# One broadcast per quad, another prologue order, early scaling of wo and wider FFN chunks in a transformer block on one core

## The chip, the cores and the metric

The kernel runs on one core of a Trainium2 chip. The core has a matrix engine (TensorE, PE in the profile), three engines for elementwise work (VectorE or DVE, ScalarE or ACT, GpSimd or POOL) and a queue engine (SyncE or SP) that issues transfers. TensorE writes its results into eight accumulator banks of 128 x 512 32-bit numbers (PSUM); everything else lives in the on-chip memory. The metric is the device time of one execution in microseconds (us); lower is better.

## The reference

One adaLN-conditioned transformer block over 2048 tokens of width 512, with 32 heads of 16 columns, and a gated FFN of width 1792:

```python
mod = (silu(c) @ w_mod).reshape(1, 6, 1, 512)        # sa, ca, ga, sb, cb, gb
h = layernorm(x) * (1 + ca) + sa
q, k, v = split_heads(h @ wqkv)                      # 32 heads, 16 columns each
p = softmax(q @ k.T * 16 ** -0.5)                    # 2048 x 2048 for each head
x = x + ga * (merge_heads(p @ v) @ wo)
h = layernorm(x) * (1 + cb) + sb
x = x + gb * ((gelu(h @ w_gate) * (h @ w_up)) @ w_down)
```

The 32 x 2048 x 2048 exponentials of the softmax are the bulk of the elementwise work.

## The kernel before

**Units and rounds.** Queries are cut into seven sets of 512, 512, 256, 256, 256, 128 and 128 tokens (`SETS`, L33). Heads are taken four at a time: a quad is the four heads that stand in the four 32-row groups of one 128-row slice, the even or the odd ones (`kme` and `kmo` hold the keys with the other heads' rows set to zero). A unit is a set and a quad; the last two sets share their first five quads. A unit is computed as the transposed scores of 128 keys by W queries; a block is 128 x 512 scores of one head. There are 2048 blocks.

**The stream** (`stream`, L1052). Six accumulator banks form two halves of three. TensorE fills one half with score blocks (`qk`), while ACT turns the other half into bf16 exponentials in one instruction of up to 1536 columns (L1167). In some rounds one of the three blocks is given to DVE instead, which computes 2 to a power by integer and polynomial steps in seven instructions (`exp_vec`, L1235): a load `dt` out of the accumulator bank, `dx`, two scalings, two products and a last combining step. ACT's instruction is then 1024 columns wide. The test that gives a block to DVE is at L1147: fewer than three such blocks under way, fewer than ten ready DVE steps in the backlog, and a side credit below 2600 (1600 near the end).

Sixteen rows of values and a column of ones (`vaug`) follow as the other product (`pv_mms`), so that each head's sum of exponentials comes out beside its output. At the end of a unit (`pv_done`, L1295), DVE copies the result to `osb`; the sums of the quad go to a scratch tensor in device memory and come back spread over all partitions (`den`); DVE takes reciprocals (`rden`); they go out to scratch again and come back as a broadcast over 32 partitions per head, in `rb`: four transfers issued by SP, each with a semaphore of its own. Then DVE multiplies `osb` by `rb` into `onorm`.

**Side work.** Projections of later slices, the output projection (`side_wo`), and the FFN of finished sets (`side_ffn`) are cut into small pieces and put between the score products. `plan` (L978) lists them with a start and a due position, and a credit lets them in. A piece of side work that waits for a DVE step holds the rest of the list. `side_ffn` computes the gate, x + 0.044715 x cubed on DVE, a tanh on ACT, the up projection, and the product, in chunks of two or more slices of 128 hidden columns (`width`, L870).

**The planner.** The program is written out ahead of time for every engine. `model` (L245) keeps a clock for each engine, with costs from `cost` (L284); each next instruction is chosen by what could run at that time. A step of DVE is put into DVE's order when its inputs are ready in this clock (`step`, L945). What the clock has wrong, the engines find out as waits, because each engine runs its instructions in the written order.

**The prologue** (`prologue`, L488) is written out by hand: loads, a warm-up of TensorE, statistics of the first tiles, `ln_rstd` on POOL (an addition and a power), normalisation on DVE, modulation columns, transposes, modulation by DVE and ACT, and K and Q of the first 512 tokens. **The tail** (`tail`, L1339) handles the last sets: `tail_den`, `tail_end` and `tail_ffn`.

**wo.** `scale_wo` (L791) multiplies the output weights by `ga` late, after the last but one set's second normalisation; earlier sets apply `ga` in `wo_fin` (L806), in a product and an addition.

Of the kernel before, what the change touches and what calls it, by code (L numbers as in the profile page):

```python
# [6 lines left out]
ALU = mybir.AluOpType  # L7
# [7 lines left out]
P = 128  # L15
# [63 lines left out]
class _Recorder:  # L79
# [165 lines left out]
    def model(self, op, t, cost):  # L245
        eng = op.eng
        if op.stream not in COMPUTE:
            self.free[eng] = t + (430 if eng == "sp" else 50)
            self.dma_free = max(t + 800, self.dma_free) + cost / 350
            op.t1 = self.dma_free + 1000  # L250
        elif eng == "pe":
            cols, rows, tp = cost
            mode = 0 if tp is None else (1 if rows == 32 else 2)
            t = max(t, self.pe_issue)
            if mode != self.pe_mode:
                t = max(t, self.pe_end + 105)
# [27 lines left out]
    def cost(self, eng, out, ins, kind):  # L284
# [6 lines left out]
        if eng == "act":  # L291
            return n * 0.833 + (51 if ps else 93)
        if eng == "pool":
            return n * (30.0 if n <= 4 else 3.0) + 200
        f = 1
# [17 lines left out]
    def act(self, out, in_, func, bias=None, scale=1.0, accum=None):  # L313
        kw = {} if bias is None else {"bias": bias}
        wr = [out]
        if accum is not None:
# [3 lines left out]
        return self.rec("act", lambda e: e.activation(out, in_, func, scale=scale, **kw), rd, wr,  # L320
                        cost=self.cost("act", out, [in_], "act"))

# [89 lines left out]
class _Kernel(_Recorder):  # L412
# [75 lines left out]
    def prologue(self):  # L488
# [30 lines left out]
        self.ts(dve, self.rm[:, 0:1], self.rm[:, 1:2], -1.0, 1.0, ALU.mult, ALU.add)  # L519

        for dc in range(NDC):
            self.mm(self.scp[:, 0, dc:dc + 1], self.crow[0:1, P * dc:P * dc + P], self.ones[0:1, 0:1])
# [10 lines left out]
        self.ln_rstd(0, 4)  # L533
        self.memset(pool, self.vaug[:, :, :].rearrange("p t (h c) -> p t h c", c=VW)[:, :, :, DH:VW], 1.0)
        self.mod_cols(self.scp[:, 1, 0:8], 0)
# [5 lines left out]
        for dc in range(NDC):  # L541
            pt = self.scp[:, 2 + dc, :].bitcast(BF16)[:, 0:512]
            for t in range(4):
                self.transpose(pt[:, P * t:P * t + P], self.tb1[:, 0, t, P * dc:P * dc + P], self.ident[:, :])
            self.modulate(dve if dc % 2 == 0 else act, self.hT[:, dc, 0:512], pt, self.modA, dc)
        for t in range(6, 8):
            self.ln_stat(t)
        self.proj_k(0, 0, self.scp[:, 2, :], "both")
        self.proj_q(0, 0, self.scp[:, 3, :], act)
        self.act_stat_fin(4, 6)  # L550
# [20 lines left out]
    def ln_rstd(self, a, b):  # L571
        r = self.rstd[:, a:b]
        self.ts("pool", r, self.mv[:, a:b, 1], EPS, None, ALU.add)
        self.tt("pool", r, r, self.half[:, 0:b - a], ALU.pow)

# [27 lines left out]

    def proj_k(self, g, dc, bank, how):
        self.proj(bank, 512 + P * dc, g)
        sl = slice(512 * g, 512 * g + 512)
        if how == "both":
            self.act(self.km[1][:, dc, sl], bank, ACT.Copy, scale=self.rm[:, 1:2])
        else:
            self.ts("dve", self.km[1][:, dc, sl], bank, self.rm[:, 1:2], None, ALU.mult)  # L610
        self.ts("dve", self.km[0][:, dc, sl], bank, self.rm[:, 0:1], None, ALU.mult)

    def proj_q(self, g, dc, bank, eng):
# [4 lines left out]
        else:  # L618
            self.ts(eng, out, bank, Q_SCALE, None, ALU.mult)

    def proj_v(self, g, dc, bank):
        for t in range(4):
            for dci in range(NDC):
                self.mm(bank[:, P * t:P * t + P], self.hT[:, dci, 512 * g + P * t:512 * g + P * t + P],
                        self.wqkv[:, dci, 1024 + P * dc:1024 + P * dc + P],
                        start=(dci == 0), stop=(dci == NDC - 1))
        dst = self.vaug[:, 4 * g:4 * g + 4, VW * 8 * dc:VW * 8 * dc + VW * 8]
        self.copy("dve", dst.rearrange("p t (h c) -> p t h c", c=VW)[:, :, :, 0:DH],
                  bank.rearrange("p (t h c) -> p t h c", t=4, c=DH))

# [160 lines left out]
    def scale_wo(self):  # L791

        if not self.dry:
            self.task([lambda qd=qd: self.tt("dve", self.wo[:, qd, :], self.wo[:, qd, :], self.ga[:, :], ALU.mult)
                       for qd in range(8)], "wo", self.after([("ln2", len(SETS) - 2)]))
        return
        yield

# [7 lines left out]
    def wo_fin(self, bank, t):  # L806
        return [lambda: self.tt("dve", self.xw[:, :], bank, self.ga[:, :], ALU.mult),
                lambda: self.tt("dve", self.xs[:, t, :], self.xs[:, t, :], self.xw[:, :], ALU.add)]

# [47 lines left out]
    def side_ffn(self, gi, part=None):  # L857
# [11 lines left out]
        chunks = []  # L869
        width = max(2, kpb)  # L870
        for a in range(0, NFC, width):
# [106 lines left out]
    def plan(self, ends, nsplit):  # L978
# [6 lines left out]
        w.append((lambda: self.side_dc(1), at(30), at(51)))  # L985
        w.append((self.side_mod, at(50), at(59)))
        w.append((lambda: self.side_dc(2), at(59), at(90)))
        w.append((lambda: self.side_q_all(1), at(90), at(105)))
# [12 lines left out]
        w.append((lambda: self.side_wo(k), s0, s0))  # L1001
        w.append((self.scale_wo, s0, s0))
        w.append((lambda: self.side_ffn(k, EARLY), s0, n - 20))
# [291 lines left out]
    def pv_done(self, rnd, acc):  # L1295
# [102 lines left out]
    def tail_end(self, k, f, l):  # L1398
# [103 lines left out]
```

## Time and profile before

| what | us |
|---|---|
| median of 3 runs | 914.01 (913.69 to 915.49) |
| the profiled execution | 912.22 |
| its span, first to last instruction | 910.5 |
| ACT busy | 877.9 (96%) |
| DVE busy | 828.2 (91%) |
| PE busy | 793.2 (87%) |
| POOL busy | 17.5 (2%) |

The granted TensorE clock was 0.995. In rows of groups, "out<-in" names the tiles written and read, "xN" counts instructions, then come the busy time in us, the mean in ns of one, and the idle time of the engine before them with what ended it. In rows of the timeline the first number is the start in us, the second the length; "x3" merges three neighbours, and brackets give the idle time before the first of them. Rows of waits give the total, the count and the longest, in us. Rows of windows give the stretch, then busy time of each engine, clock, share of busy DMA engines and GB/s. A line such as L320 or L332 is that of a helper that records many kinds of work; the tiles tell them apart.

### The profile page before, as it was taken

The numbers are of one execution on the slowest core, as the hardware profiler recorded it, in microseconds if no ns is written. First come the engines' busy times: TensorE is split into PE (matmuls) and PEld (weight loads), VectorE is DVE, ScalarE is ACT, GpSimd is POOL, SyncE is SP. The second block draws the span as 40 slices with busy tenths as digits, with TensorE's granted clock in tenths as the row PEclk, the third lists the DMA queues.
The fourth block names the chain that finished last, engine by engine and source line by source line (L and its number), as shares of the span: only waits on it lengthen the run. The fifth ranks groups of instructions, "written<-read, shape, count | busy, mean of one in ns | idle before, by whom it ended". The sixth has DMA issues, their size and how long they took to land.

```text
span 910.5 us, 20673 instructions
## 1 busy us (share of the span) xinstructions
PE 793.2 (87%) x8566; PEld 290.2 (32%) x8700; DVE 828.2 (91%) x2031; ACT 877.9 (96%) x756; POOL 17.5 (2%) x34
## 2 busy tenths in 40 slices
PE   7899898888898889888888898998889889888887
PEld 3333322322222222222223232333333334234455
DVE  7778999999998999999998999999999899878964
ACT  5999999999999999999999999999999999999992
POOL 2100000000000000000000000000000000000000
PEclk9999999999999999999999999999999999999999
DMA  9002220000100000000000000000000000000000
GB/s 300 1 25 80 93 71 13 13 15 13 54 14 10 5 13 14 13 14 25 20 14 14 14 8 13 19 21 20 15 8 20 20 8 14 20 15 14 20 9 13
DMA packets 35336, 25.18 MB, mean 28 GB/s; under 512 B 19053, under 2 KB 31082, under 8 KB 35242
## 3 DMA queue, kind: packets, MB, share of 16 engines
q1 hardware_dynamic: 32858, 22.28, 8.5%
q10 hardware_dynamic: 2384, 1.57, 0.6%
q8 instruction: 68, 1.11, 0.5%
q14 instruction: 26, 0.21, 0.1%
HBM read 21.23 MB, written 2.61 MB: 26 GB/s over the span
## 4 chain that ended last, share of the span: by engine, by line
ACT 73%; DVE 11%; PE 8%; DMA 5%; SPq 1%; issue 1%; POOL 1%; DVEq 0%
ACT E L320 70%; PE ps_sc L307 4%; PE ps_mi L307 3%; ACT wreg L320 2%; DMA rb<-scr_rec 2%; DMA scr_rec<-rden 2%; SPq L370 1%; PE ps_pv L307 1%; DVE dt L332 1%; DVE qT L324 1%; DVE qT L337 1%; DVE dx L332 1%; DMA den<-scr_den 1%; DVE osb L341 1%; DVE onorm L324 1%
## 5 line engine op out<-in xcount | busy, mean ns | idle before, releaser
L320 ACT ACTIVATE E<-ps_sc 128x1536 bf16<-128x1536 f32 (+2 forms) x698 | 850.1, 1415 | 13.4 <-PE ps_sc L307 12.7
L307 PE MATMUL ps_pv<-E,vaug 128*17 128x256 bf16 (+2 forms) x2908 | 181.7, 301 | 3.7 <-DVE osb L341 2.1
L307 PE MATMUL ps_sc<-qT,kmo 32*128 32x256 bf16 (+2 forms) x1664 | 164.9, 299 | 22.4 <-ACT E L320 17.0
L307 PE MATMUL ps_sc<-qT,kme 32*128 32x256 bf16 (+2 forms) x1600 | 166.6, 304 | 19.0 <-ACT E L320 12.8
L332 DVE TENSOR_SCALAR dt<-ps_sc 128x512 int32<-128x512 f32 x190 | 130.3, 687 | 6.5 <-PE ps_sc L307 3.9
L307 PE MATMUL ps_sc<-kme,ident 128*128 128x512 bf16 x289 | 94.0, 384 | 41.2 <-ACT E L320 37.7
L307 PE MATMUL ps_mi<-wreg,mreg 128*128 128x256 bf16 (+2 forms) x603 | 112.6, 305 | 10.3 <-DVE wreg L341 4.6
L307 PEld LDWEIGHTS ps_sc<-qT,kmo 32*128 32x128 bf16 x1664 | 48.4, 92 | 123.6 <-ACT E L320 69.5
L307 PEld LDWEIGHTS ps_sc<-qT,kme 32*128 32x128 bf16 x1600 | 47.3, 92 | 126.6 <-ACT E L320 75.7
L307 PEld LDWEIGHTS ps_pv<-E,vaug 128*17 128x17 bf16 x2908 | 52.5, 88 | 99.7 <-issue 86.1
L324 DVE TENSOR_TENSOR qT<-qT,dx 128x512 f16<-128x512 f16 x190 | 79.2, 421 | 1.1
L332 DVE TENSOR_SCALAR dx<-dt 128x512 f16<-128x512 uint16 x190 | 78.8, 420 | 0.1
L307 PEld LDWEIGHTS ps_mi<-wreg,mreg 128*128 128x128 bf16 x624 | 49.7, 97 | 56.7 <-issue 23.1
L337 DVE SCALAR_TENSOR_TENSOR qT<-dt,qT 128x512 int16<-128x512 int32 x95 | 65.1, 686 | 0.3
L307 PE MATMUL ps_mi<-dreg,hreg 128*128 128x512 bf16 x184 | 56.7, 384 | 2.7 <-issue 1.7
L324 DVE TENSOR_TENSOR ed<-ed,dx 128x512 f16<-128x512 f16 x128 | 53.3, 420 | 0.8
L307 PEld LDWEIGHTS ps_sc<-kme,ident 128*128 128x128 bf16 x327 | 23.1, 97 | 91.9 <-ACT E L320 89.7
L337 DVE SCALAR_TENSOR_TENSOR ed<-dt,ed 128x512 int16<-128x512 int32 x64 | 43.9, 686 | 0.3
L341 DVE CAST wreg<-ps_mi 128x512 bf16<-128x512 f32 x51 | 35.1, 687 | 8.8 <-PE ps_mi L307 8.4
L324 DVE TENSOR_TENSOR wreg<-wreg 128x512 bf16<-128x512 bf16 (+1 forms) x74 | 38.5, 520 | 0.4
L307 PE MATMUL ps_mi<-wo,onorm 128*128 128x512 bf16 x107 | 33.1, 391 | 3.4 <-DVE rb L344 1.7
L307 PE MATMUL ps_mi<-hreg,wreg 128*128 128x512 bf16 x106 | 34.1, 385 | 2.3 <-issue 0.8
(129 smaller groups left out, 765.5 us busy)
## 6 DMA issues: line engine op xcount, KB each, us to landing
rb<-scr_rec SPq DMA_DIRECT2D x64, 64.0 KB, 2.0
rb<-scr_rec SPq DMA_DIRECT2D x116, 32.0 KB, 1.8
mreg<-in_w_mod_dram SPq DMA_DIRECT2D x1, 2048.0 KB, 14.5
out_dram<-xs SPq DMA_DIRECT2D x16, 128.0 KB, 1.7
mreg<-in_B_w_gate_dram SPq DMA_DIRECT2D x4, 448.0 KB, 5.7
mreg<-in_B_w_up_dram SPq DMA_DIRECT2D x4, 448.0 KB, 4.0
dreg<-in_B_w_down_dram SPq DMA_DIRECT2D x3, 512.0 KB, 4.6
wreg<-in_A_wqkv_dram SPq DMA_DIRECT2D x3, 384.0 KB, 10.6
```

The source lines that it names most:

```text
L307: return self.rec("pe", lambda e: e.matmul(out, lhsT, rhs, start=start, stop=stop, tile_position=tp), [lhsT, rhs], [out], cost=(n, int(rhs ...
L320: return self.rec("act", lambda e: e.activation(out, in_, func, scale=scale, **kw), rd, wr, cost=self.cost("act", out, [in_], "act"))
L324: return self.rec(eng, lambda e: e.tensor_tensor(out, a, b, op), [a, b], [out], cost=self.cost(eng, out, [a, b], "tt"))
L332: return self.rec(eng, lambda e: e.tensor_scalar(out, a, s1, s2, **kw), rd, [out], cost=self.cost(eng, out, [a], "ts" if len(rd) == 1 else ...
L337: return self.rec("dve", lambda e: e.scalar_tensor_tensor(out, a, s, b, op0=op0, op1=op1), rd, [out], cost=self.cost("dve", out, [a, b], " ...
L341: return self.rec(eng, lambda e: e.tensor_copy(out, in_), [in_], [out], cost=self.cost(eng, out, [in_], "ts"))
L370: return e.dma_start(out, in_)
```

## The change

- `fin1`: one transfer with a source of [4, 32, W] replaces the four broadcasts of a quad.
- `model`: a transfer starts 1600 ns after its issue in the planner's clock instead of 800, so each lands 0.8 us later in it. `cost`: ACT with a bias column costs 190 ns more; POOL's power and its small addition have prices of their own.
- `prologue`: the memset of the ones in `vaug` on POOL goes ahead of the first `ln_rstd`. The transposes use banks 5 to 2 in place of 2 to 5. K of the first group: ACT writes the even keys, Q goes to DVE, and DVE writes the odd keys after that; before, ACT wrote the odd keys, DVE the even ones after ACT, and ACT Q. The statistics of tiles 6 and 7 move from ahead of K to behind this.
- `scale_wo` moves in `plan` from the end to the place after `side_mod`, and holds the side queue until its eight products are done. `wo_fin` becomes one addition from the accumulator bank. `tail_end` waits for `wo` no more.
- `side_ffn`: sets of 256 queries use chunks of four slices (1024 columns) instead of two (512), where the set isn't the one computed in part.
- `tail_end`: of four modulations, two move from ACT to DVE.
- `proj_k` and `proj_v` are gone; the latter was not called.

```diff
@@ model
-            self.dma_free = max(t + 800, self.dma_free) + cost / 350
+            self.dma_free = max(t + 1600, self.dma_free) + cost / 350
             op.t1 = self.dma_free + 1000
@@ cost
-            return n * 0.833 + (51 if ps else 93)
+            return n * 0.833 + (51 if ps else 93) + (190 if kind == "col" else 0)
         if eng == "pool":
-            return n * (30.0 if n <= 4 else 3.0) + 200
+            return {"pow": 160.0 * n + 380, "small": 270}.get(kind, 3.0 * n + 200)
@@ prologue
+        self.memset(pool, self.vaug[:, :, :].rearrange("p t (h c) -> p t h c", c=VW)[:, :, :, DH:VW], 1.0)
+
         for dc in range(NDC):
             self.mm(self.scp[:, 0, dc:dc + 1], self.crow[0:1, P * dc:P * dc + P], self.ones[0:1, 0:1])
...
         self.ln_rstd(0, 4)
-        self.memset(pool, self.vaug[:, :, :].rearrange("p t (h c) -> p t h c", c=VW)[:, :, :, DH:VW], 1.0)
         self.mod_cols(self.scp[:, 1, 0:8], 0)
...
-            pt = self.scp[:, 2 + dc, :].bitcast(BF16)[:, 0:512]
+            pt = self.scp[:, 5 - dc, :].bitcast(BF16)[:, 0:512]
...
+        bank = self.scp[:, 5, :]
+        self.proj(bank, 512, 0)
+        self.act(self.km[0][:, 0, 0:512], bank, ACT.Copy, scale=self.rm[:, 0:1])
+        self.proj_q(0, 0, self.scp[:, 4, :], dve)
+        self.ts(dve, self.km[1][:, 0, 0:512], bank, self.rm[:, 1:2], None, ALU.mult)
         for t in range(6, 8):
             self.ln_stat(t)
-        self.proj_k(0, 0, self.scp[:, 2, :], "both")
-        self.proj_q(0, 0, self.scp[:, 3, :], act)
         self.act_stat_fin(4, 6)
@@ scale_wo
             self.task([lambda qd=qd: self.tt("dve", self.wo[:, qd, :], self.wo[:, qd, :], self.ga[:, :], ALU.mult)
-                       for qd in range(8)], "wo", self.after([("ln2", len(SETS) - 2)]))
-        return
-        yield
+                       for qd in range(8)], "wo")
+        yield from self.until("wo")
@@ wo_fin
-        return [lambda: self.tt("dve", self.xw[:, :], bank, self.ga[:, :], ALU.mult),
-                lambda: self.tt("dve", self.xs[:, t, :], self.xs[:, t, :], self.xw[:, :], ALU.add)]
+        return [lambda: self.tt("dve", self.xs[:, t, :], self.xs[:, t, :], bank, ALU.add)]
@@ side_ffn
-        width = max(2, kpb)
+        width = max(2, kpb if part is not None else 1024 // W)
@@ plan
         w.append((self.side_mod, at(50), at(59)))
+        w.append((self.scale_wo, at(59), at(59)))
         w.append((lambda: self.side_dc(2), at(59), at(90)))
...
-        w.append((self.scale_wo, s0, s0))
@@ pv_done, fin1
-            for j in range(4):
-                self.dma("sp", self.rb[32 * j:32 * j + 32, lo:hi],
-                         s2[W * j:W * j + W].rearrange("(o n) -> o n", o=1).broadcast_to([32, W]), "dd%d%d" % (sem, j))
+            self.dma("sp", self.rb[:, lo:hi],
+                     s2.rearrange("(j o n) -> j o n", j=4, o=1).broadcast_to([4, 32, W]), "dd%d" % sem)
@@ tail_end
-        yield from self.until("wo")
         yield lambda: self.mm(bank, self.ident[:, :], self.xs[:, tile, :], start=True, stop=False)
...
-                self.modulate("act", self.t2T[:, dc, c0:c0 + W],
+                self.modulate("act" if i == 0 else "dve", self.t2T[:, dc, c0:c0 + W],
                               pb.bitcast(BF16)[:, W * i:W * i + W], self.modB, dc)
```

More of the change, by code (lines that the diff above doesn't have):

```diff
@@ L320, in act @@
         return self.rec("act", lambda e: e.activation(out, in_, func, scale=scale, **kw), rd, wr,
-                        cost=self.cost("act", out, [in_], "act"))
+                        cost=self.cost("act", out, [in_], "act" if bias is None else "col"))
     def tt(self, eng, out, a, b, op):
@@ L572, in ln_rstd @@
         r = self.rstd[:, a:b]
-        self.ts("pool", r, self.mv[:, a:b, 1], EPS, None, ALU.add)
-        self.tt("pool", r, r, self.half[:, 0:b - a], ALU.pow)
+        v, h = self.mv[:, a:b, 1], self.half[:, 0:b - a]
+        self.rec("pool", lambda e: e.tensor_scalar(r, v, EPS, None, op0=ALU.add), [v], [r], cost=self.cost("pool", r, [v], "small"))
+        self.rec("pool", lambda e: e.tensor_tensor(r, r, h, ALU.pow), [r, h], [r], cost=self.cost("pool", r, [r], "pow"))
     def ln_norm(self, t, dst, src=None):
@@ L602, in proj @@
                     start=(dci == 0), stop=(dci == NDC - 1))
[L604 to L611, printed above, removed]
     def proj_q(self, g, dc, bank, eng):
@@ L619, in proj_q @@
             self.ts(eng, out, bank, Q_SCALE, None, ALU.mult)
[L621 to L629, printed above, removed]
     def done(self, key):
```

## The prediction

> **What bounds the kernel now.** I read the page from the top: shares of the engines, the chain, the costliest groups, then who waited for whom.
>
> ```profile
> PE 793.2 (87%) x8566; PEld 290.2 (32%) x8700; DVE 828.2 (91%) x2031; ACT 877.9 (96%) x756; POOL 17.5 (2%) x34
> ACT E L320 70%; PE ps_sc L307 4%; PE ps_mi L307 3%; ACT wreg L320 2%; DMA rb<-scr_rec 2%; DMA scr_rec<-rden 2%; SPq L370 1%; PE ps_pv L307 1%; DVE dt L332 1%; DVE qT L324 1%; DVE qT L337 1%; DVE dx L332 1%; DMA den<-scr_den 1%; DVE osb L341 1%; DVE onorm L324 1%
> ACT E L320 <- PE ps_sc L307: 12.7, 18, 2.1
> DVE onorm L324 <- DMA rb<-scr_rec: 11.0, 14, 2.1
> ```
>
> The exponentials on ACT bound it: 96% busy, 70% of the chain, and only 12.7 us of waiting before them. So only four things shorten the program: an earlier first exponential, less ACT work between first and last, fewer idle moments of ACT, and a shorter tail. DVE takes some of the 2048 blocks of 512 columns; its free time counts as far as it takes more. Rows of the timeline and of the groups by shape give the prices:
>
> ```profile
> 17.23 3.71 ACT L320 ACTIVATE E<-ps_sc 128x1536 bf16<-128x1536 f32 x3 [0.58 <-PE ps_sc L307]
> 883.80 0.72 ACT L320 ACTIVATE wreg<-wreg 128x512 bf16<-128x512 bf16 x1
> 884.33 1.54 ACT L320 ACTIVATE E<-ps_sc 128x1536 bf16<-128x1536 f32 x1
> L320 ACT ACTIVATE E<-ps_sc 128x1536 bf16<-128x1536 f32 x474 | 685.9, 1555 | 5.4 <-PE ps_sc L307 4.8
> L320 ACT ACTIVATE E<-ps_sc 128x1024 bf16<-128x1024 f32 x218 | 243.2, 1135 | 1.6 <-PE ps_sc L307 1.5
> 850.12 0.42 DVE L324 TENSOR_TENSOR xs<-xs,xw 128x512 bf16<-128x512 bf16 x1
> 850.46 0.42 DVE L324 TENSOR_TENSOR qT<-qT,dx 128x512 f16<-128x512 f16 x1
> 850.80 0.29 DVE L332 TENSOR_SCALAR ed<-dx 128x512 f16<-128x512 f16 x1
> 851.00 0.28 DVE L332 TENSOR_SCALAR qT<-qT 128x512 f16<-128x512 f16 x1
> 851.54 0.68 DVE L332 TENSOR_SCALAR dt<-ps_sc 128x512 int32<-128x512 f32 x1
> ```
>
> ACT does 474x3+218x2=1858 blocks, DVE the other 190. A block that DVE takes shortens one exponential from 1555 to 1135 ns: 0.42 us of ACT. A DVE step overlaps the next by 0.08 (0.42 long, 0.34 from start to start). So a block costs DVE 0.60 (dt), 0.34 (dx, as a product), two products of 0.34, two scalings of 0.20 and a last step like dt: 2.6 us.
>
> **The change part by part.** *The Pool memset of vaug goes ahead of the first rstd.*
>
> ```profile
> 2.55 0.15 DVE L332 TENSOR_SCALAR rm<-rm 128x1 f32<-128x1 f32 x1
> 3.71 0.69 DVE L360 BATCH_NORM_STATS2 st<-xs 128x6 f32<-128x512 bf16 x1 [1.01 <-DMA xs<-in_A_x_dram]
> 8.70 2.28 POOL L348 MEMSET vaug<- 128x512 bf16 x1
> L332 DVE TENSOR_SCALAR dreg<-xs,mv,rstd x4: 396/404/2340, 8.8 to 11.7; 128x512 bf16<-128x512 bf16 x4
> 10.34 0.38 PE L307 MATMUL ps_mi<-dreg 128*128 128x512 bf16 x1
> 12.14 1.31 PEld L311 LDWEIGHTS ps_sc<-ident,dreg 128*128 128x128 bf16 x13 [0.22 <-DVE dreg L332]
> ```
>
> One of the four normalisations took 2340 ns instead of about 400, and it ended as the memset did (8.70+2.28): the two stood in each other's way. Without it they end at about 10.1, so TensorE, through with the warm-up at 10.6, is the next to be late. The fourth transpose, at 12.14 before, comes three loads of 0.10 after 10.6, at 10.9: 1.25 us earlier, and modulation, K, Q and the first exponential move with it. At its new place the memset runs at about 2.2 to 4.4, where DVE does little. If it holds up the small rm step at 2.55, the statistics start at 4.5 instead of 3.7, rstd comes 0.8 later, and the fourth transpose at 11.0. Bounds 0 (something else is late) and -1.25; I take -1.2, by the slow normalisation.
> [...]
>
> *K and Q of the first group.* ACT writes the even keys, DVE the queries, and the odd keys follow. Statistics of tiles 6 and 7 move from ahead of K to behind all that.
>
> ```profile
> 13.79 0.69 DVE L360 BATCH_NORM_STATS2 st<-xs 128x6 f32<-128x512 bf16 x1
> 15.19 0.69 ACT L320 ACTIVATE kmo<-ps_sc,rm 128x512 bf16<-128x512 f32 x1 [0.66 <-PE ps_sc L307]
> 15.98 0.75 DVE L332 TENSOR_SCALAR kme<-ps_sc,rm 128x512 bf16<-128x512 f32 x1 [0.50 <-ACT kmo L320]
> 16.05 0.60 ACT L320 ACTIVATE qT<-ps_sc 128x512 bf16<-128x512 f32 x1 [0.18 <-PE ps_sc L307]
> 18.68 1.06 DVE L332 TENSOR_SCALAR dreg<-xs,mv,rstd 128x512 bf16<-128x512 bf16 x3 [1.49 <-POOL rstd L324]
> 30.36 0.09 PEld L307 LDWEIGHTS ps_sc<-qT,kmo 32*128 32x128 bf16 x2 [0.87 <-ACT E L320]
> ```
>
> Before, the even keys ended at 16.73. Now the queries end last, at 16.05 plus some 0.69 on DVE, the same time: 0. But the two statistics, hidden under the projection at 13.79 to 15.48, now follow about 0.7 of odd keys, so rstd of group 1 comes some 2.4 later than it would, 1.1 later in absolute time, while its keys are wanted 1.2 earlier. The cover is thin: the first scores on group 1, at 30.36, waited 0.87 for ACT and not for keys. The Pool price in the planner helps, since DVE need not sit 1.49 at 18.68. Bounds 0 and +2.4; I take +0.4, near the cover.
>
> *Wider chunks for 256 queries.* Seven chunks of 512 columns become 1024, 1024, 1024 and 512, in three sets: nine pairs become one. A pair of tanh costs ACT 2x0.53 (883.80 to 884.33); a wide one costs this:
>
> ```profile
> 575.76 0.94 ACT wreg L320
> L324 DVE TENSOR_TENSOR wreg<-wreg 128x1024 bf16<-128x1024 bf16 x28 | 19.2, 685 | 0.0
> 876.62 1.09 DVE L324 TENSOR_TENSOR wo<-wo,ga 128x512 bf16<-128x512 bf16 x3
> ```
>
> That is 0.12 less, nine times: -1.0 (bounds -0.8 and -1.1 by rounding). DVE has four steps per chunk. A wide product takes 685 ns, 0.60 without the overlap; two narrow ones 2x0.34. That saves 0.07, and the other three steps about as much: 0.28 a pair, 2.5 us in all.
>
> *wo scaled early.* Each of 15 tiles drops the separate addition (0.34 at 850.12): -5.1 us of DVE. Eight scalings of 0.34, +2.7, come into the stream from the last 35 us (876.62), where no block is given to DVE any more. They hold the side queue until done: K, Q, V of the third quarter stand behind, with some 30 blocks until they are due. DVE gains 5.1+2.5-2.7=4.9 us: 1.9 blocks, -0.8 us of ACT. Bounds 0 (the planner takes none) and -2.8: 6.7 blocks, if the 11.0 us of waits for rb and the 1.49 at 18.68 are used too.
>
> *One broadcast per quad, later landings.* SP issues 47 instead of 188, 0.42 each (317/421/1588 below). What stands behind them on SP (the next denominators, output rows) goes sooner. The planner puts three small transfers 0.8 later each, so it sets the product with rb some 2 us later in DVE's order.
>
> ```profile
> L370 SPq DMA_DIRECT2D rb<-scr_rec x188: 317/421/1588, 75.8 to 883.2; - x188
> rb<-scr_rec SPq DMA_DIRECT2D x116, 32.0 KB, 1.8
> 616.50:621.00 4.50, 4.45 (x51) 1.61 (x52) 3.92 (x10) 4.25 (x4) 0.00 (x0) 1.00 0.18 58
> 785.93 0.43 DVE L324 TENSOR_TENSOR onorm<-osb,rb 128x256 bf16<-128x256 f32 x1 [1.72 <-DMA rb<-scr_rec]
> 790.77 1.02 ACT L320 ACTIVATE E<-ps_sc 128x1024 bf16<-128x1024 f32 x1 [0.81 <-PE ps_sc L307]
> 792.83 2.79 ACT L320 ACTIVATE E<-ps_sc 128x1536 bf16<-128x1536 f32 x2 [1.03 <-PE ps_sc L307]
> 868.97 0.29 DVE L324 TENSOR_TENSOR onorm<-osb,rb 128x128 bf16<-128x128 f32 x1 [2.09 <-DMA rb<-scr_rec]
> 871.82 12.20 ACT L320 ACTIVATE E<-ps_sc 128x1536 bf16<-128x1536 f32 x9 [1.30 <-PE ps_sc L307]
> ```
>
> The two longest waits (1.72, 2.09) were each followed by ACT running dry: 0.81+1.03 and 1.30. All of it is 3.1; the second follows directly through recip and wo products, the first less surely. The merged landing isn't in the trace. The window moved 256 KB (this broadcast and an output row) in 0.18x4.5x16=13 us of DMA-engine time, so a 128 KB quad is 6.5. A 32 KB one lands after 1.8, of which 6.5/4/16=0.1 is moving: 1.7 stays. On 16 engines the quad lands after 1.7+0.4=2.1; before, the fourth landed 1.3+1.8=3.1 after the first issue. The planner's 2 us cover waits of 0.8 in the mean (11.0 over 14), so I take -2.6, near the full effect; bounds are 0 and -3.1, and what a later landing adds is a rival.
> [...]
>
> *The tail.* Four modulations on ACT become two there and two on DVE.
>
> ```profile
> 894.45 1.01 DVE L337 SCALAR_TENSOR_TENSOR hreg<-ps_sc,E 128x512 bf16<-128x512 f32 x2
> 894.92 1.50 ACT L320 ACTIVATE wreg<-ps_sc,modB 128x128 bf16<-128x128 bf16 x4 [0.39 <-PE ps_sc L311]
> 896.13 3.93 PE L307 MATMUL ps_sc<-wreg,mreg 128*128 128x128 bf16 x62
> ```
>
> DVE is free of the gated products at 895.46, so the last modulation ends near 896.0 instead of 896.42; TensorE, busy from 896.13 almost to the end, is late next. -0.4 (bounds 0 and -1.0). The bank order, the removed dead functions and the Pool and ACT prices cost nothing by themselves: they only reorder.
>
> Sum: -1.2+0.4-1.0-0.8-2.6-0.4=-5.6. The profiled execution took 912.22; the median of the runs, 914.01, lies 1.8 above. So 906.6 in a profile, 908.4 as a median.
>
> **The rivals.** *More blocks go to DVE.* For it: 11.0 us of waits are freed and wide chunks leave fewer steps in the backlog, whose limit is ten steps and not microseconds. Against: waits don't exist in the planner's clock. Term -2.8 instead of -0.8: 906.4.
> *The merged transfer lands late.* If only four engines carry it, 128 KB land 1.7+6.5/4=3.3 us after issue and 256 KB (512 queries) 1.7+13/4=5.0, where the fourth landed some 3.1 to 3.3 after the first issue. The waits for rb then stay and the rb term goes; with one wait more like that at 868.97 (1.30 of dry ACT) the sum is -5.6+2.6+1.3=-1.7: 912.3. For it: a quad's source has only four rows of its own; against: the planner's 2 us.
> *DVE gets fewer blocks* and the kernel is slower. Place: the test before a block, which refuses it while side credit is over 2600 (1600 late). A side queue that stands still, for eight scalings or for a wide chunk's tanh, lets credit grow. Each block lost costs 0.42. My gain is gone at 13 fewer of 190 and it is slower by over 0.2% at 18; at 22, +3.6: 917.6. For it: twelve wider or narrower chunks, each with a longer stop; against: the next chunk's gate runs during the stop.
>
> **How the numbers follow.** My case 0.48 (905.5 to 911), more blocks 0.22, late landing 0.14, fewer blocks 0.16. A measurement tells 0.2%, 1.8 us. Faster: 0.48+0.22+half of the late landing=0.77; same 0.08; slower 0.15. The lower bounds of all terms add to -9.3, 904.7; with the 0.7 by which the fastest run shown lies under the median (913.69 to 915.49), 904. Upwards, 916 takes in the late landing and the milder half of the lost blocks.
>
> **What would show it.** Four normalisations of 400 ns near 8.8; first exponential near 16.0; no wait on ACT between 20 and 40; nine more tanh of 1024 columns; 192 dt loads; waits for rb under 3 us in total; ACT's waits before ps_sc near 9. It would be wrong if dt loads fall below 180, or if ACT's waits before ps_sc exceed the 12.7 of now.

## The result and the profile after

| | before | after |
|---|---|---|
| median of the runs | 914.75 (913.69 to 917.80, 4 runs) | 907.27 (906.24 to 907.74, 4 runs) |
| ratio | | 0.9911 [0.9885, 0.9938] |
| the profiled execution; its span | 912.22; 910.5 | 907.0; 905.3 |
| granted clock, mean | 0.995 | 1.000 |

The kernel is 0.9% faster, close to the 908.4 that was forecast. The profiles differ by 5.2 us, the medians by 7.5: the profiled execution of before lies 2.5 under the median of its runs, that of after at its own. Part of the larger difference can be the clock: of the 28 other executions of the kernel before, timed beside the experiments, the five with a mean granted clock of 0.997 or 0.998 took 912.0 to 914.4 us, the thirteen with 0.990 to 0.994 took 913.6 to 919.1. The shares of the engines and the chain of after, from the page:

```profile
PE 796.2 (88%) x8565; PEld 291.3 (32%) x8700; DVE 817.4 (90%) x1976; ACT 876.5 (97%) x744; POOL 16.2 (2%) x34
ACT E L320 72%; PE ps_sc L307 4%; DMA rb<-scr_rec 4%; PE ps_mi L307 3%; ACT wreg L320 2%; DVE dt L332 2%; DMA scr_rec<-rden 2%; PE ps_pv L307 1%; DVE qT L332 1%; DVE dx L332 1%; DVE ed L324 1%; DVE ed L337 1%; DVE qT L324 1%; DVE qT L337 1%; DVE mreg L324 0%
```

The bound is what it was: exponentials on ACT. DVE does 10.8 us less, but the share of "DMA rb<-scr_rec" in the chain rose from 2% to 4%. The waits of after (total, count, longest, in us) agree:

```profile
ACT E L320 <- PE ps_sc L307: 12.1, 17, 2.1
DVE onorm L324 <- DMA rb<-scr_rec: 10.4, 9, 2.0
```

Before these were 12.7 and 11.0. Neither fell as forecast (near 9, and under 3). The first holds the prologue and the tail too; between the first and the last exponential alone, ACT's gaps fell from 6.35 to 4.26 us.

I cut both spans at the start of the first exponential of the stream and at the end of the last. The prologue went from 17.23 to 15.26 (-2.0), the stream from 870.5 to 868.4 (-2.1), the tail from 22.8 to 21.6 (-1.1). The prologue of after, from the timeline:

```profile
2.08 2.26 POOL L348 MEMSET vaug<- 128x512 bf16 x1
2.55 0.15 DVE L332 TENSOR_SCALAR rm<-rm 128x1 f32<-128x1 f32 x1
8.85 1.38 DVE L332 TENSOR_SCALAR dreg<-xs,mv,rstd 128x512 bf16<-128x512 bf16 x4 [1.49 <-POOL rstd L579]
14.08 0.69 DVE L332 TENSOR_SCALAR qT<-ps_sc 128x512 bf16<-128x512 f32 x1 [2.02 <-PE ps_sc L307]
15.26 1.45 ACT L320 ACTIVATE E<-ps_sc 128x1536 bf16<-128x1536 f32 x1 [1.36 <-PE ps_sc L307]
```

Four normalisations take 1.38 us together, and the rm step still starts at 2.55 while the memset runs. The first exponential comes 0.7 earlier than forecast, most of which the windows explain (the third number from the end is the granted clock). Before:

```profile
11.00:13.00 2.00, 1.66 (x12) 1.16 (x13) 1.86 (x7) 0.10 (x1) 0.00 (x0) 0.58 1.10 344
```

After:

```profile
11.00:13.00 2.00, 1.87 (x17) 0.84 (x15) 1.00 (x2) 1.45 (x2) 0.00 (x0) 1.00 1.10 345
```

Before, TensorE had half its clock for one stretch of 3.41 us from 11.3; after, it had all of it. The groups by shape of the stream of after:

```profile
L320 ACT ACTIVATE E<-ps_sc 128x1536 bf16<-128x1536 f32 x475 | 685.2, 1563 | 5.2 <-PE ps_sc L307 4.9
L320 ACT ACTIVATE E<-ps_sc 128x1024 bf16<-128x1024 f32 x217 | 244.3, 1145 | 0.5 <-PE ps_sc L307 0.3
L320 ACT ACTIVATE wreg<-wreg 128x1024 bf16<-128x1024 bf16 x23 | 26.7, 1160 | 0.0
L332 DVE TENSOR_SCALAR dt<-ps_sc 128x512 int32<-128x512 f32 x189 | 129.8, 688 | 8.9 <-PE ps_sc L307 6.4
```

The wide tanh went from 14 to 23, the nine pairs of the forecast. From start to start of its neighbours a wide one costs ACT 0.948 us and a narrow one 0.521, so nine pairs save 0.84 (starts read from the trace). But the blocks on DVE went from 190 to 189, not to 192.

The tail changed in a way that I hadn't looked for. The last steps of DVE before, from the timeline:

```profile
904.54 0.42 DVE L337 SCALAR_TENSOR_TENSOR hreg<-ps_sc,E 128x256 bf16<-128x256 f32 x1 [1.10 <-PE ps_sc L307]
906.52 0.42 DVE L324 TENSOR_TENSOR xs<-xs,xw 128x512 bf16<-128x512 bf16 x1
907.77 0.43 DVE L324 TENSOR_TENSOR xs<-xs,xw 128x512 bf16<-128x512 bf16 x1
```

And after:

```profile
891.83 0.69 DVE L332 TENSOR_SCALAR wreg<-ps_sc,modB 128x128 bf16<-128x128 bf16 x2 [0.76 <-PE ps_pv L307]
893.15 0.43 DVE L324 TENSOR_TENSOR xs<-xs,xw 128x512 bf16<-128x512 bf16 x1
900.64 0.42 DVE L337 SCALAR_TENSOR_TENSOR hreg<-ps_sc,E 128x256 bf16<-128x256 f32 x1 [1.10 <-PE ps_sc L307]
902.62 0.42 DVE L324 TENSOR_TENSOR xs<-xs,xw 128x512 bf16<-128x512 bf16 x1
```

Before, the rows of both last sets were finished at the very end, one behind the other. After, one of them is through at 893 and only one is left.

### The profile page after: what moved, and what is told of

It reads as the page before. It is cut to its first block, busy times and chain, and to the rows that moved or that the text cites. A ratio compares the mean times of both kernels' runs of the same rounds, so it can differ in the third digit from the quotient of the medians.

```text
span 905.3 us, 20373 instructions
## 1 busy us (share of the span) xinstructions
PE 796.2 (88%) x8565; PEld 291.3 (32%) x8700; DVE 817.4 (90%) x1976; ACT 876.5 (97%) x744; POOL 16.2 (2%) x34
## 3 DMA queue, kind: packets, MB, share of 16 engines
q8 instruction: 68, 1.11, 0.5%
## 4 chain that ended last, share of the span: by engine, by line
ACT 74%; DVE 11%; PE 8%; DMA 5%; issue 1%; POOL 0%
ACT E L320 72%; PE ps_sc L307 4%; DMA rb<-scr_rec 4%; PE ps_mi L307 3%; ACT wreg L320 2%; DVE dt L332 2%; DMA scr_rec<-rden 2%; PE ps_pv L307 1%; DVE qT L332 1%; DVE dx L332 1%; DVE ed L324 1%; DVE ed L337 1%; DVE qT L324 1%; DVE qT L337 1%; DVE mreg L324 0%
## 5 line engine op out<-in xcount | busy, mean ns | idle before, releaser
L320 ACT ACTIVATE E<-ps_sc 128x1536 bf16<-128x1536 f32 (+2 forms) x698 | 849.2, 1425 | 12.5 <-PE ps_sc L307 12.1
L307 PE MATMUL ps_sc<-qT,kme 32*128 32x256 bf16 (+2 forms) x1600 | 170.2, 304 | 20.6 <-ACT E L320 13.2
L307 PE MATMUL ps_sc<-qT,kmo 32*128 32x256 bf16 (+2 forms) x1664 | 168.4, 298 | 17.3 <-ACT E L320 12.8
L307 PE MATMUL ps_sc<-kme,ident 128*128 128x512 bf16 x299 | 96.3, 384 | 39.0 <-ACT E L320 33.4
L307 PE MATMUL ps_mi<-wreg,mreg 128*128 128x256 bf16 (+2 forms) x605 | 115.8, 306 | 5.9 <-DVE wreg L337 2.2
L337 DVE SCALAR_TENSOR_TENSOR wreg<-wreg,ps_mi 128x512 bf16<-128x512 bf16 x51 | 34.8, 683 | 2.2 <-ACT wreg L320 1.1
L307 PE MATMUL ps_pv<-qT,vaug 128*17 128x256 bf16 (+2 forms) x166 | 36.1, 290 | 0.0
```

Of the source, the lines that this page charges most:

```text
L307: return self.rec("pe", lambda e: e.matmul(out, lhsT, rhs, start=start, stop=stop, tile_position=tp), [lhsT, rhs], [out], cost=(n, int(rhs ...
L337: return self.rec("dve", lambda e: e.scalar_tensor_tensor(out, a, s, b, op0=op0, op1=op1), rd, [out], cost=self.cost("dve", out, [a, b], " ...
```

## The experiments

My theory was that of the prediction: the merged broadcast and the later landings together free DVE of its waits. The main rival was that the merged transfer lands late and only the planner's later landings help. All kernels but `e10_before_1600` start from the changed one. `e12_800_fill` to `e15_priced_narrow` ran on another chip than the other experiments; each ratio is to executions of the kernel before on the same chip. Times in us; first exponential, gaps (of ACT between the first and the last exponential) and waits for rb are of the profiled execution.

| kernel | median (range) | ratio to before | span | first exp. | gaps | rb waits (count) | blocks |
|---|---|---|---|---|---|---|---|
| changed | 907.27 (906.24 to 907.74) | 0.9911 [0.9885, 0.9938] | 905.3 | 15.26 | 4.26 | 10.4 (9) | 189 |
| e2_four | 904.15 (903.51 to 904.95) | 0.9871 [0.9849, 0.9894] | 901.8 | 15.35 | 1.97 | 0 | 190 |
| e3_800 | 942.95 (940.90 to 946.57) | 1.0297 [1.0257, 1.0337] | 942.1 | 15.70 | 35.66 | 43.9 (35) | 192 |
| e10_before_1600 | 909.44 (908.87 to 909.62) | 0.9938 [0.9919, 0.9957] | 907.2 | 16.60 | 3.60 | 0 | 189 |
| e11_priced | 901.66 (901.43 to 902.21) | 0.9855 [0.9834, 0.9876] | 899.9 | 15.34 | 0.75 | 1.3 (2) | 189 |
| e12_800_fill | 958.27 (957.82 to 961.38) | 1.0496 [1.0472, 1.0519] | 956.1 | 16.34 | 41.79 | 45.4 (33) | 191 |
| e1_memset_late | 908.13 (907.68 to 908.86) | 0.9915 [0.9893, 0.9937] | 907.0 | 17.54 | 4.01 | 10.1 (9) | 189 |
| e5_kq_old | 908.03 (905.92 to 910.23) | 0.9913 [0.9882, 0.9945] | 908.1 | 16.26 | 7.53 | 11.1 (10) | 192 |
| e7_wo_late | 912.21 (909.04 to 912.66) | 0.9961 [0.9944, 0.9978] | 909.0 | 15.35 | 8.08 | 8.5 (8) | 190 |
| e13_priced_wo_late | 904.41 (904.18 to 905.10) | 0.9896 [0.9882, 0.9911] | 903.4 | 16.41 | 2.36 | 3.3 (2) | 190 |
| e14_priced_tail_act | 902.32 (902.06 to 902.73) | 0.9873 [0.9858, 0.9888] | 900.5 | 16.21 | 0.41 | 0.4 (1) | 189 |
| e6_narrow | 908.02 (906.99 to 911.44) | 0.9928 [0.9904, 0.9951] | 905.7 | 15.42 | 3.08 | 7.7 (8) | 187 |
| e15_priced_narrow | 904.10 (902.63 to 904.40) | 0.9889 [0.9874, 0.9903] | 902.4 | 16.27 | 1.11 | 1.4 (2) | 188 |

### One transfer or four, later landings or not

The four broadcasts come back; the later landings stay.

```diff
@@ fin1
-            self.dma("sp", self.rb[:, lo:hi],
-                     s2.rearrange("(j o n) -> j o n", j=4, o=1).broadcast_to([4, 32, W]), "dd%d" % sem)
+            for j in range(4):
+                self.dma("sp", self.rb[32 * j:32 * j + 32, lo:hi],
+                         s2[W * j:W * j + W].rearrange("(o n) -> o n", o=1).broadcast_to([32, W]), "dd%d%d" % (sem, j))
```

> The changed kernel with four broadcasts per quad again, the later landings kept. Theory 'later landings in the planner': the last packet of a 512-query quad comes 2.9 us after the first issue instead of 4.6, DVE's waits for rb fall from 10.4 to under 5 us, ACT's waits in the stream stay at or below the 4.3 us of the changed kernel, and the median is 906 to 907.5. Rival 'one transfer did it': SP is slow again, waits for rb and ACT's waits go back to 11.0 and 6.4 us, and the median is 909 to 910.

It is faster than the changed kernel, and than the 906 to 907.5 us expected: no wait for rb is left, and ACT's gaps fall from 4.26 to 1.97. The intervals of the two ratios just touch, but all runs of `e2_four` lie under all of the changed kernel. On the same chip `e1_memset_late` and `e5_kq_old`, which keep the merged transfer, took 908.13 and 908.03; less the 1.2 to 1.3 us of its late memset (below), the first still leaves 2.7. So the merging costs some 3 us: 2.7 by that run, 3.1 by the medians, 3.5 by the spans. Why shows where little else moves data. The changed kernel issued this quad of 512 queries at 324.30 (timeline and windows; in the windows the number before the last is the share of the 16 DMA engines that is busy):

```profile
324.30 0.53 SPq L370 DMA_DIRECT2D rb<-scr_rec  x1
325.00:326.00 1.00, 0.90 (x9) 0.24 (x9) 1.00 (x3) 1.00 (x2) 0.00 (x0) 1.00 0.13 31
326.00:327.00 1.00, 1.00 (x6) 0.26 (x6) 0.97 (x4) 1.00 (x2) 0.00 (x0) 1.00 0.24 92
327.00:328.00 1.00, 0.71 (x8) 0.19 (x7) 0.96 (x2) 1.00 (x2) 0.00 (x0) 1.00 0.26 100
328.00:329.00 1.00, 0.47 (x5) 0.21 (x3) 0.00 (x0) 1.00 (x2) 0.00 (x0) 1.00 0.10 39
329.26 0.69 DVE L324 TENSOR_TENSOR onorm<-osb,rb 128x512 bf16<-128x512 f32 x1 [1.30 <-DMA rb<-scr_rec]
```

The same in `e2_four`:

```profile
316.26 1.71 SPq L370 DMA_DIRECT2D rb<-scr_rec  x4
317.00:318.00 1.00, 0.84 (x14) 0.28 (x10) 1.00 (x2) 1.00 (x2) 0.00 (x0) 1.00 0.32 119
318.00:319.00 1.00, 1.00 (x7) 0.33 (x7) 1.00 (x4) 1.00 (x1) 0.00 (x0) 1.00 0.51 133
319.00:320.00 1.00, 1.00 (x9) 0.22 (x11) 0.94 (x3) 1.00 (x2) 0.00 (x0) 1.00 0.11 27
rb<-scr_rec SPq DMA_DIRECT2D x64, 64.0 KB, 2.1
```

The merged transfer holds a quarter of the engines, 4 of 16 (busy share 0.24 and 0.26 in its two full windows, against up to 0.51 with four transfers), for work of the same order (the four windows add to 0.73 us of all engines, the three to 0.94: 12 and 15 us of one engine). DVE got its data 4.96 us after the issue; by the packets of the 16 quads of 512 queries, the last ended 4.62 after the issue in the median, against 2.89 (before) and 3.04 (`e2_four`) after the first of four issues. What makes it four no run shows: the merged source is [4, 32, W] wherever there is one. The planner prices the same transfer, 256 KB over 350 bytes per ns, at 0.75 us.

Now the reverse: the merged transfer with the old landing time.

```diff
@@ model
-            self.dma_free = max(t + 1600, self.dma_free) + cost / 350
+            self.dma_free = max(t + 800, self.dma_free) + cost / 350
```

> The changed kernel with 800 instead of 1600 ns in the planner, the single broadcast kept. Theory 'later landings': DVE's waits for rb rise from 10.4 to 20 us or more, ACT runs dry 2 us more, and the median is 909 to 911. Rival 'one transfer did it': waits for rb under 14 us and the median within 1 us of the changed kernel.

3% slower than before. I had the direction right and the size far off (909 to 911 expected). Waits of this kernel, and one place of its timeline and windows:

```profile
DVE onorm L324 <- DMA rb<-scr_rec: 43.9, 35, 4.8
ACT E L320 <- PE ps_sc L307: 39.3, 42, 5.1
121.71 0.69 DVE L324 TENSOR_TENSOR onorm<-osb,rb 128x512 bf16<-128x512 f32 x1 [4.84 <-DMA rb<-scr_rec]
122.92 0.75 DVE L332 TENSOR_SCALAR kme<-ps_mi,rm 128x512 bf16<-128x512 f32 x1
121.00:124.00 3.00, 0.00 (x0) 0.00 (x0) 2.29 (x4) 1.21 (x1) 0.00 (x0) 0.77 0.61 199
124.00:127.00 3.00, 2.62 (x17) 1.52 (x17) 3.00 (x9) 0.00 (x0) 0.00 (x0) 0.50 0.01 3
127.28 2.52 ACT L320 ACTIVATE E<-ps_sc 128x1536 bf16<-128x1536 f32 x2 [5.08 <-PE ps_sc L307]
```

DVE stands 4.84 us; the casts of the keys stand behind it; TensorE has nothing for 3 us and comes back at half clock (0.50 from 124 to 127); ACT is dry for 5.08. Here the transfer was late beyond its own slowness: it was issued at 115.24, three loads of `w_down` from 115.83 on, and the busy share of the 16 engines was 0.79 from 117 to 119 and about 1 from 119 to 122. So the merged transfer without the later landings would have been far slower than before: the planner's 0.8 us are what keeps the edit a gain. Alone on the kernel before:

```diff
@@ model (kernel before)
-            self.dma_free = max(t + 800, self.dma_free) + cost / 350
+            self.dma_free = max(t + 1600, self.dma_free) + cost / 350
```

> The kernel before with only the later landings (1600 ns) in the planner. Theory 'later landings': DVE's waits for rb go from 11.0 us to under 2, ACT's waits in the stream from 6.4 to under 3, and the median is 3 to 5 us under that of before (ratio 0.995 to 0.997). Rival 'a new order by chance': ratio within 0.002 of 1, the waits move elsewhere.

All 14 waits for rb go, and the kernel gains 0.62% [0.43, 0.81], somewhat more than expected. That is some two thirds of the whole change's 0.89%.

If the price is what is wrong, a right one should bring both. The merged transfer stays, and the planner is told 3.1 times its bytes, 2.3 us for 512 queries instead of 0.75:

```diff
@@ fin1
-            self.dma("sp", self.rb[:, lo:hi],
-                     s2.rearrange("(j o n) -> j o n", j=4, o=1).broadcast_to([4, 32, W]), "dd%d" % sem)
+            dst, src = self.rb[:, lo:hi], s2.rearrange("(j o n) -> j o n", j=4, o=1).broadcast_to([4, 32, W])
+            self.rec("sp", lambda e: e.dma_start(dst, src), [src], [dst], dma="dd%d" % sem, cost=3.1 * 4 * P * W)
```

> The changed kernel with one broadcast per quad, but its transfer priced 3.1 times as long in the planner (2.3 us instead of 0.75 for 512 queries). Theory 'late merged landing, planner's price': DVE's waits for rb, 10.4 us in the changed kernel, fall under 3 us, ACT's waits in the stream to about 2.0, and the median comes within 1 us of the kernel with four broadcasts (904 to 905.5, ratio to before near 0.988). Rival 'four transfers are better in themselves' (SP, queues): the median stays at 907 or more.

The best version of the study, 901.66, under the 904 to 905.5 expected and faster than both kernels: its interval ends at 0.9876, the changed kernel's begins at 0.9885. From `e2_four` the intervals don't tell it apart. Its chain on the page, and its waits:

```profile
ACT E L320 87%; ACT wreg L320 3%; PE ps_sc L307 2%; PE ps_mi L307 2%; PE ps_pv L307 1%; DMA rb<-scr_rec 1%; DMA xs<-in_A_x_dram 0%; DVE st L360 0%; DVE dt L332 0%; DMA scr_rec<-rden 0%; DVE vaug L341 0%; ACT hreg L320 0%; DVE wreg L337 0%; DVE kme L332 0%; DVE kmo L332 0%
ACT E L320 <- PE ps_sc L307: 8.8, 8, 2.1
DVE onorm L324 <- DMA rb<-scr_rec: 1.3, 2, 1.1
```

The exponentials are 87% of the chain instead of 72%, and ACT's gaps in the stream are 0.75 us. The transfer itself is the same; only its time in the planner's clock is another.

### Is it the wait or the clock?

The stretches of half clock in the streams made me ask whether TensorE's clock, rather than the wait itself, dries ACT. So in `e3_800` more filler matmuls were to keep TensorE busy:

```diff
@@ (on e3_800)
-FILL = 4600
+FILL = 6000
```

> One broadcast with 800 ns landings (the slow kernel of 942 us), and the planner's filling rule raised from 4600 to 6000 columns of TensorE work in 3413 ns. Theory 'waits for rb lower the TensorE clock': the waits for rb stay near 40 us, but the stretches at half clock (41 us of the stream in the slow kernel) mostly go and ACT's waits fall from 35.7 to 15 to 20 us: 922 to 930 us. Rival 'the waits alone': half clock or not, ACT's waits and the time stay within 4 us of 942.

A miss: 958.27. The fillers doubled (676 instead of 342), half clock in the stream fell from 41.0 us to 17.1, and yet the gaps grew to 41.79, of which only 10.97 lay in half clock or up to 2 us behind it (18.87 of 35.66 in `e3_800`). The fillers themselves held TensorE for 213.8 us instead of 111.9, so the run doesn't separate the two. What share of the loss is the clock's stays open.

### The prologue

The memset goes back behind the first rstd:

```diff
@@ prologue
-        self.memset(pool, self.vaug[:, :, :].rearrange("p t (h c) -> p t h c", c=VW)[:, :, :, DH:VW], 1.0)
...
         self.ln_rstd(0, 4)
+        self.memset(pool, self.vaug[:, :, :].rearrange("p t (h c) -> p t h c", c=VW)[:, :, :, DH:VW], 1.0)
```

> The changed kernel with the memset of vaug back behind the first rstd, all else as changed. Theory 'blocked normalisation': one normalisation takes some 2.3 us again, the first exponential starts at 16.5 to 17.2 instead of 15.26, and the median is 1.2 to 2 us above the changed kernel, 908.5 to 909.3, if the memset made most of the 1.97 us. Rival 'order of K and Q': the first exponential stays below 15.8 and the time within 0.6 us of the changed kernel.

One normalisation takes 2336 ns again, and the first exponential is at 17.54. But TensorE also had half clock from 12.1 to 15.5 in this execution, so it stands beside the four kernels that had the memset early and half clock too, at 16.21 to 16.41: 1.1 to 1.3 later. At full clock, 16.60 in `e10_before_1600`, with the memset late and the old order of K and Q, stands beside 15.26 to 15.42 in five kernels with both new: 1.2 to 1.3. The median, 908.13, is only 0.9 above the changed kernel's, less than expected, and the intervals overlap.

A sixth kernel at full clock, `e3_800`, starts at 15.70, and the clock isn't why. TensorE's products for the modulation columns, in the changed kernel and then in `e3_800`:

```profile
9.41 0.94 PE L307 MATMUL ps_sc<-sc_bf,mreg 128*128 128x1 bf16 x32 [1.03 <-DVE dreg L332]
9.84 0.94 PE L307 MATMUL ps_sc<-sc_bf,mreg 128*128 128x1 bf16 x32 [0.71 <-DVE dreg L332]
```

They read `w_mod`, whose load of 1024 KB took 7.6 us from issue to landing in the first and 8.0 in the second; in all 14 profiles they start 0.13 to 0.14 us after it has landed. (The normalisation that the row names had ended at 9.15 in `e3_800`.) In all six kernels the first exponential starts 5.85 to 5.86 us behind these products. With the slow normalisation gone, the load of `w_mod` sets the start.

The old banks, the old order of K, Q and statistics, the memset early:

```diff
@@ prologue
-            pt = self.scp[:, 5 - dc, :].bitcast(BF16)[:, 0:512]
+            pt = self.scp[:, 2 + dc, :].bitcast(BF16)[:, 0:512]
...
-        bank = self.scp[:, 5, :]
-        self.proj(bank, 512, 0)
-        self.act(self.km[0][:, 0, 0:512], bank, ACT.Copy, scale=self.rm[:, 0:1])
-        self.proj_q(0, 0, self.scp[:, 4, :], dve)
-        self.ts(dve, self.km[1][:, 0, 0:512], bank, self.rm[:, 1:2], None, ALU.mult)
         for t in range(6, 8):
             self.ln_stat(t)
+        bank = self.scp[:, 2, :]
+        self.proj(bank, 512, 0)
+        self.act(self.km[1][:, 0, 0:512], bank, ACT.Copy, scale=self.rm[:, 1:2])
+        self.ts(dve, self.km[0][:, 0, 0:512], bank, self.rm[:, 0:1], None, ALU.mult)
+        self.proj_q(0, 0, self.scp[:, 3, :], act)
```

> The changed kernel with the old banks and the old order of K, Q and the statistics of tiles 6 and 7 in the prologue, the memset still early. Theory 'blocked normalisation': the first exponential stays at 15.2 to 15.5, since keys and queries ended together before. Rival 'order of K and Q': it starts at 15.9 or later, 0.7 us being from this order. Both: the statistics are back under the projection, and the wait of DVE before Q (2.02 us) goes.

First exponential at 16.26, where the rival had it, but again with half clock from 10.8. The new order with half clock gave 16.21 to 16.41 (`e12_800_fill`, `e13_priced_wo_late`, `e14_priced_tail_act`, `e15_priced_narrow`). Counted from the products for the modulation columns it is 6.89 us with the old order and 6.90 with the new one in all four, so the order is worth nothing by itself. The span of 908.1 is no effect of the order either: 6.28 of its 7.53 us of gaps lie in or just behind three stretches of half clock at 96.1, 126.8 and 468.2, each behind a wait for rb of over 2 us.

### wo, the modulations, the chunks

wo is scaled late again, and the earlier sets apply `ga` tile by tile:

```diff
@@ plan, scale_wo, wo_fin, tail_end
-        w.append((self.scale_wo, at(59), at(59)))
+        w.append((self.scale_wo, s0, s0))
...
-        return [lambda: self.tt("dve", self.xs[:, t, :], self.xs[:, t, :], bank, ALU.add)]
+        return [lambda: self.tt("dve", self.xw[:, :], bank, self.ga[:, :], ALU.mult),
+                lambda: self.tt("dve", self.xs[:, t, :], self.xs[:, t, :], self.xw[:, :], ALU.add)]
...
+        yield from self.until("wo")
```

> The changed kernel with wo scaled late and ga applied tile by tile, as before. Theory 'DVE work': DVE has 2.4 us more in the stream; at most one or two blocks fewer (0.4 to 0.8 us of ACT), and the tail grows by up to 1 us by the eight products: 0.5 to 1.8 us slower than the changed kernel, ratio 0.992 to 0.9935. Rival 'idle DVE': blocks and time don't change, since DVE has free time (87.9 us idle).

> The kernel with the priced broadcast (901.66 us), with wo scaled late and ga applied tile by tile. Theory 'early scaling shortens the tail': the stretch from the last exponential to the end grows from 21.85 to 22.7 us or more, the stream by 0 to 0.8 us: 902.5 to 903.8 us. Rival 'DVE work in the stream': the tail stays under 22.2 and DVE takes two or more blocks less.

The first has it on the changed kernel, the second on `e11_priced`. Both tails are 22.75 us long against 21.63 and 21.85, and the order of before is back: in the second kernel the two last sums on DVE stand at 899.41 and 900.67, in `e11_priced` at 887.76 and 897.23. So the early scaling is worth 0.9 us in the tail. DVE does 190 blocks in both, one more than with early scaling and not fewer, and both kernels are slower than expected: 4.9 us above the changed kernel instead of 0.5 to 1.8, and 904.41 instead of 902.5 to 903.8. The whole of it is 0.5% on the changed kernel and 0.4% on the priced one, but 4 of the first one's 8.08 us of gaps are in or behind half clock, and 1.07 of the second's 3.5 us is a prologue at half clock.

Four modulations on ACT, on `e11_priced`:

```diff
@@ tail_end
-                self.modulate("act" if i == 0 else "dve", self.t2T[:, dc, c0:c0 + W],
+                self.modulate("act", self.t2T[:, dc, c0:c0 + W],
```

> The kernel with the priced broadcast, all four last modulations on ACT. Theory of the prediction: the tail grows by 0.4 us, to 22.2 or more. Rival 'TensorE is late anyway': the tail stays within 0.15 us of 21.85.

The tail is 22.10 against 21.85, between the two expectations: the split is worth 0.25. The times of the two kernels don't tell them apart. ACT's four take 1.50; with the split the last ends on DVE, which starts 0.56 behind ACT.

Chunks of 512 columns again, on the changed kernel and on `e11_priced`:

```diff
@@ side_ffn
-        width = max(2, kpb if part is not None else 1024 // W)
+        width = max(2, kpb)
```

> The changed kernel with chunks of 512 columns for 256 queries again. Theory 'tanh and DVE steps': 14 wide and 23 narrow tanh as before, ACT +0.8 us, DVE +2.5 us or one block less: 1 to 1.7 us slower than the changed kernel, ratio near 0.993. Rival 'longer stops of the side queue': DVE takes three or more blocks more with narrow chunks and the median is equal or lower.

> The kernel with the priced broadcast, chunks of 512 columns for 256 queries. Theory 'tanh and DVE steps': the stream grows by 0.8 us through tanh and by 0.4 for each block less; 902.5 to 904 us. Rival 'longer stops of the side queue': DVE takes more blocks with narrow chunks, and the time is the same within 0.5 us.

On the changed kernel the spans are 0.4 apart, and the intervals overlap, so the 1 to 1.7 us expected isn't shown there. On the priced one, with few gaps to blur it, the stream is 1.65 longer: 0.84 for nine more pairs of tanh, 0.43 for one block fewer on DVE, 0.36 of gaps.

## Why the prediction was right

The sum was -5.6 against the profiled execution; the spans differ by -5.2. That it came so near is partly luck: the clock of the prologue and the early end of one set in the tail, which it didn't have, gave 0.7 and 0.9 us, and about as much was missing from the blocks (1.2), the broadcast (0.5) and a rest without a name (0.4). Its terms:

| step | forecast | measured | from |
|---|---|---|---|
| memset | -1.2 | -1.2 to -1.3 | first exponential at full clock |
| K and Q order | 0 | 0 | half-clock prologues, old and new |
| statistics late | +0.4 | 0 | ACT's first wait after 20 us is 0.24, at 84.64 |
| clock in the prologue | none | -0.7 | rest of -1.97 |
| wider tanh | -1.0 | -0.84 | 9 pairs |
| blocks to DVE | -0.8 | +0.4 | 189 dt loads |
| broadcast, landings | -2.6 | -2.1 | ACT's gaps |
| tail | -0.4 | -1.1 | tail of the span |
| unassigned | | +0.4 | |

**The prologue** went as argued: the slow normalisation was the memset's, the rm step was not held, and transposes, K and Q followed by the full 1.2. Beside the late memset one normalisation took 2340 ns (before) and 2336 (`e1_memset_late`); beside the early one, which ran from 2.08 to 4.34, the rm step at 2.55 took 0.15 as before. TensorE was the next to be late, as forecast, but it waits for the load of `w_mod`. The cover under the late statistics was thicker than I took it for.

**The step that failed is "One broadcast per quad, later landings".** Its size was nearly right, -2.1 for -2.6 if the whole fall of ACT's gaps is put down to it, its cause half wrong. I took 16 engines, 2.1 us to landing, and waits under 3 us. The transfer takes four engines (busy share 0.24 to 0.26 of 16) and some 5 us for 512 queries (4.62 to the last packet in the median, 4.96 to the product shown), as the second rival had it, and DVE still waits 10.4 us. The waits only moved: six of the nine are now at quads of 512 queries. The rival's price, 912.3, failed as well, since it let the whole term go with the waits; none of the waits left is over 2.05 us, and in this execution none was followed by a stretch of half clock, as that at 785.93 before had been. Taken apart, the later landings give 0.62% and the merging takes some 0.4% back.

**"wo scaled early"** had the freed time about right (DVE is 10.8 us less busy; less 1.9 of the slow normalisation and some 2.6 of the block that it no longer takes, with 0.7 for the two modulations that it took over, that is 7.0 against 5.1+2.5=7.6) and its use wrong: the planner gave DVE one block fewer. Narrow chunks give 187 and 188, so the wide ones bring one or two, and the rest of the freed time went to nothing. Of the two bounds I gave, 0 would have been the better value.

**"The tail"** was mis-sized: I counted the split of the modulations (0.4; it measured 0.25) and not that early scaling lets one of the last two sets end 9 us ahead of the other (0.9).

## What to carry to other kernels

Where a program is written out ahead, the price that the planner gives a transfer decides as much as the transfer: with the merged broadcast 3.9% of the time before lay between 1600 and 800 ns in one number (0.62% with four), and 0.56% more in pricing one kind of transfer at 3.1 times its bytes. When you merge small transfers, read the share of busy DMA engines in a quiet window of the profile: here the merged one kept 0.24 to 0.26 of them busy, the four up to 0.51. Compare prologues only at the same granted clock, and with the same landing of the load that they wait for.

## What the runs showed of the hardware

In these traces TensorE's granted clock fell to half (0.50) for stretches of 3.41 us (or twice that), in the middle of a stream that kept TensorE busy (87% of the span before). The one in the stream before, in the windows:

```profile
786.00:789.50 3.50, 2.02 (x30) 0.65 (x30) 3.50 (x10) 3.45 (x4) 0.00 (x0) 1.00 0.00 0
789.50:793.00 3.50, 3.43 (x24) 0.65 (x24) 3.26 (x9) 1.66 (x3) 0.00 (x0) 0.51 0.16 42
```

DVE's wait of 1.72 us ended at 785.93; TensorE was short of work until 789.5 (2.02 of 3.50), then ran at 0.51, and ACT stood still for 0.81 and 1.03 us although the wait was over. Over all profiles there are 17 such stretches in the streams; 16 have a wait for rb of 1.6 us or more in the 9 us ahead, one (in `e7_wo_late`, at 132.4) has none, and not every such wait has one behind it (2.05 us at 89.43 in the changed kernel has none, nor the longest of `e1_memset_late`, 2.9). So the wait alone doesn't decide. TensorE's own busy time does better. Within an execution, the changes of the clock lie whole multiples of 3.413 us apart (before, those up to the end of the stream are at 4.51, 11.34, 14.75, 789.58 and 792.99). Cut into windows on that grid, the streams of the 14 profiles have 3524 at full clock. In the 17 of them that half clock followed, TensorE was busy for 24 to 59% of the window; of the other 3507, four were under 60%. (The page of after counts 8565 matmuls beside 8700 weight loads; if records of matmuls are missing, a share reads too low.) The window ahead of the stretch in `e7_wo_late`, and that stretch:

```profile
128.96:132.37 3.41, 2.00 (x15) 0.49 (x7) 3.41 (x9) 3.11 (x3) 0.00 (x0) 1.00 0.00 0
132.37:135.78 3.41, 3.41 (x15) 0.58 (x14) 2.38 (x7) 1.78 (x2) 0.00 (x0) 0.50 0.02 5
```

The prologues agree. The seven with half clock had TensorE busy for 50 to 62% of the window ahead of it; in the other seven no window of the prologue from the first at full clock on is under 68%. The grid lies differently in each execution. Where it gave full clock for the first time at 3.95 to 4.51 us, the warm-up was through early and TensorE stood 1.2 to 1.4 us until `w_mod` had landed; where that was at 5.00 or later, 0.1 to 1.0 us (in `e1_memset_late`, at 5.24, the late memset added a second pause). The window in which the normalisations begin, before and after:

```profile
7.92:11.34 3.42, 1.71 (x36) 1.02 (x35) 2.56 (x2) 0.91 (x4) 3.06 (x2) 1.00 1.16 298
8.41:11.82 3.41, 2.34 (x50) 2.00 (x51) 2.48 (x8) 1.10 (x3) 0.40 (x1) 1.00 1.17 299
```

This sets the prologue's 15.26 to 15.42 in five executions apart from its 16.21 to 16.41 in four. It is still read from executions that differ in other ways too; no run was made to set the share. The window ahead needn't be idle: half clock followed windows in which TensorE was busy for up to 59% in the streams and 62% in the prologues.
